# Attention with beacon keys, then an ELU feed-forward: key and query transposes by DMA, loads issued by ScalarE, fillers in the head, smaller first tiles

## The chip, the cores and the metric

The kernel runs on one core of one Trainium2 chip. The metric is the device time of one execution in microseconds (us); it is taken as the median of several runs. The profile is of one execution of its own, with a span from the first to the last instruction and a device time beside it. TensorE is called PE in the profile, VectorE DVE, ScalarE ACT, GpSimd POOL and SyncE SP; SPq, ACTq and POOLq are the instruction queues from which these engines issue DMAs.

## The reference

There are 8 batches of 8 heads, 576 tokens and 64 dimensions per head. 16 beacon keys and values stand ahead of the 576 of each head and are seen by every query; the others are causal. The attention's output, 4608 tokens by 512, goes through a feed-forward of 2048 with an ELU.

```python
scores = (q @ k_all.T) / sqrt(64)              # k_all: 16 beacon keys, then 576 keys
scores[:, 16:] = where(causal, -1e9, scores)   # the beacon columns stay open
a = softmax(scores);  x = a @ v_all            # per batch and head
x = x.transpose(0, 2, 1, 3).reshape(4608, 512)
h = x @ w_in                                   # 512 -> 2048
out = where(h > 0, h, exp(min(h, 0)) - 1) @ w_out
```

## The kernel before

**Attention.** Heads go in pairs: pair n is batch b = n // 4, heads 2·hp and 2·hp + 1. `load_pair` brings keys and queries of a pair into one staging tile `st32` (keys on even partitions, queries on odd), nine consecutive tokens per partition and head, so in rows of 2304 bytes. `cast_pair` makes it bf16 (`st16`), and TensorE transposes it in nine matmuls against an identity, with a tenth for the beacon keys (`do_T`, and `do_T2` for batch 0, which uses other PSUM buffers). VectorE copies the keys from PSUM to `kT` (`do_kT`), VectorE or ScalarE the queries to `qT` (`do_qT`). `do_SC` computes scores with keys on partitions (tile `sc`), `do_exp` applies the exponential on ScalarE (`et`), `do_mask` zeroes the causal part on GpSimd, `do_AV` multiplies by V (`av`, with a column of ones for the sums), and `do_norm` divides into `x16`. From batch 2 on `turn_x` transposes `x16` into `xT` by DMA on SP, five per batch; batches 0 and 1 do it on TensorE (`do_xT`).

V is loaded by `load_v` in five chunks of 128 keys per batch, in rows of 256 bytes, and cast by `cast_v`. Staging buffers: four `st32`, two `st16`, five `vst`, one `bk32` for the beacon keys.

**Feed-forward.** Tokens go in tiles, two of 256 and then eight of 512. `do_mm1` computes 512 columns of `hps` by 4 matmuls of 512 (or 8 of 256) columns; `do_e` (ScalarE), `do_clamp` (GpSimd) and `do_join` (VectorE) make the ELU, and `do_mm2` multiplies by `w_out16` into `ops` for 128 tokens at a time, which VectorE copies to `osb` and SP stores. The weights come by eight DMAs from GpSimd's queue, which cast to fp16 (`load_w`), each after a mask that `W_AFTER` names.

**Order.** Nothing in this is left to a run-time scheduler. `Plan` takes every step as an `Op` with an engine, a key, a duration, what it depends on and which buffers it takes and gives, steps through a modelled time, and emits the instructions of each engine in the order that comes out. PE, DVE, ACT, POOL and SP are engines of this plan, and so is a single server "DMA". The keys come from tables (`SHIFT`, `AT`, `AT0`, `PACES`) that set where each batch and each tile lies. `FIRST` gives the order of the first loads. On the chip each engine runs its instructions in that order and waits for semaphores. DMAs from SP and ScalarE share eight semaphores in turn: a DMA waits until the one eight places before it has landed.

```python
slots = {"sc": 2, "ff": 4, "av": 2, "ops": 1, "et": NET, "rl": 2, "e": NE, "gt": NG, "osb": 3,
         "st": 4, "sb": 2, "bk": 1, "vst": 5}
plan = Plan(slots, {"PE": 16.0})
```

"ff" are the four PSUM buffers that `hps`, `av`, `xt` and `ops` take in turn; "sc" are two double buffers for scores, and for the transposes of `do_T`.

Of the kernel before, what the change touches and what calls it, by code (L numbers as in the profile page):

```python
# [10 lines left out]
FP32 = mybir.dt.float32  # L11
FP16 = mybir.dt.float16
BF16 = mybir.dt.bfloat16
AFT = mybir.ActivationFunctionType
ALU = mybir.AluOpType
P = 128


class Op:
    def __init__(self, eng, key, dur, fn, deps=(), take=(), give=(), mode=None, lat=0.03):  # L20
        self.eng, self.key, self.dur, self.fn = eng, key, dur, fn
        self.deps, self.take, self.give = [d for d in deps if d is not None], take, give
        self.mode, self.lat = mode, lat
        self.left, self.after = 0, []


class Plan:
# [10 lines left out]
    def run(self):  # L38
# [9 lines left out]
        free = dict.fromkeys(pending, 0.0)  # L48
        mode = None
        for op in self.ops:  # L50
            if not op.left:
                heapq.heappush(ready[op.eng], (op.key, op.seq))
        events, order, now, n_left, tick = [], [], 0.0, len(self.ops), 0
        while n_left:
            for eng in ready:
                if free[eng] > now + 1e-9:
                    continue
                line = pending[eng]
# [16 lines left out]
                for item in skipped:  # L75
                    heapq.heappush(ready[eng], item)
                if op is None:
                    continue
                for t in op.take:
# [14 lines left out]
            while events and events[0][0] <= now + 1e-9:  # L94
                _, _, op = heapq.heappop(events)
                if op is None:
                    continue
                n_left -= 1
                for t in op.give:
                    self.slots[t] += 1  # L100
                for o in op.after:
                    o.left -= 1
                    if not o.left:
                        heapq.heappush(ready[o.eng], (o.key, o.seq))
        self.length = now
# [7 lines left out]
def kernel(  # L113
# [23 lines left out]

    TILES = [(0, 256), (256, 512)] + [(t, t + TTS) for t in range(TTS, NT, TTS)]
    NTT = len(TILES)
# [59 lines left out]

    NG, NET, NKQ = 20, 8, 4  # L200
    konst = ctx.enter_context(tc.tile_pool(name="konst", bufs=1))
# [20 lines left out]
    x16s = [big.tile([P, NKC, DM], FP16, name=f"x16_{i}") for i in range(2)]  # L222
    kTs = [big.tile([P, SKP], BF16, name=f"kT_{i}") for i in range(NKQ)]
    qTs = [big.tile([P, S], BF16, name=f"qT_{i}") for i in range(NKQ)]
    et_bufs = [big.tile([P, 2, 512], FP16, name=f"et_{i}") for i in range(NET)]
# [4 lines left out]
    with tc.tile_pool(name="psum", bufs=1, space=bass.MemoryType.PSUM) as psum:  # L230
# [3 lines left out]
            "sc": 2, "ff": 4, "av": 2, "ops": 1, "et": NET, "rl": 2, "e": NE, "gt": NG, "osb": 3,  # L234
            "st": 4, "sb": 2, "bk": 1, "vst": 5,
        }
        plan = Plan(slots, {"PE": 16.0})
        add = plan.add

# [3 lines left out]

        def load(key, dur, fn, deps=(), take=(), issue=0.47):

            issue = add("SP", key, issue, fn, deps=deps, take=take)
            issues.append(issue)
            return add("DMA", key, dur, None, deps=[issue], lat=2.0)

        issues = []  # L250
        add("SP", -1e6, 0.8, None)
# [3 lines left out]
        def load_bk(b):  # L255
            t = bks[b] = stage.tile([P, DM], FP32, tag="bk", name="bk32", bufs=1)
            nc.sync.dma_start(
                out=t[0:NB].rearrange("n (h d) -> n h d", h=H), in_=beacon_k[b].rearrange("h n d -> n h d"))
# [13 lines left out]
        def cast_pair(n, eng):  # L272
# [4 lines left out]
            else:  # L277
                eng.tensor_copy(out=dst, in_=src)  # L278

        def turn_x(b, blk):  # L280
            q0, rows, _ = BLOCKS[blk]
            nc.sync.dma_start_transpose(  # L282
                out=xTa[:, :, b * S + q0:b * S + q0 + rows], in_=x16s[b % 2][0:rows, blk, :])

        def load_v(b, jc):
            vst = vsts[b, jc] = stage.tile([P, H, D], FP32, tag="vst", name="vst", bufs=5)
            if jc == 0:
                nc.sync.dma_start(out=vst[0:NB], in_=beacon_v[b].rearrange("h n d -> n h d"))
            r0 = NB if jc == 0 else 0
            lo = P * jc - NB + r0  # L290
            n = kc_sz[jc] - r0
            nc.sync.dma_start(out=vst[r0:r0 + n], in_=v[b, :, lo:lo + n, :].rearrange("h s d -> s h d"))

# [190 lines left out]
        def do_store(tt, t4):  # L484
# [4 lines left out]

        SHIFT = [18.19, -1.67, -5.21, 9.28, 2.92, -5.56, -3.02, 18.21]  # L490
        AT = [-2.75, -0.54, -0.93, -0.06, 0.2, 1.01, 1.99, -16.61]
        AT0 = [[-45.78, -33.15, -38.79, -34.41], [-45.52, -23.75, -37.77, -41.96], [-33.6, -16.81, -31.44, -41.61]]
        PACES = [(-10.52, 1.48, 24.15, -2.31), (-10.42, 4.31, 27.52, 4.6), (37.71, 0.81, 11.65, 4.01), (83.94, 2.16, 31.7, 1.22), (112.53, 2.24, 29.18, 2.45)]
        W_AFTER = [[21.51, 12.09, 17.39, 6.76], [7.67, 24.47, 24.74, 25.24]]
        ON_POOL = "20010220"
        X_ON_ACT = "00"
        LAG = 17.55
        URGE = 72.32
        Q_ON_ACT = "01111110"
        FIRST = (  # L500
            "q2 k1 q1 v2 v1 k2 k3 q3 q5 v0 q4 k4 k5 v4 b1 v3 k6 q6 v6 v5 v9 q7 k7 v8 v7 ").split()

# [14 lines left out]
        def plan_loads(n):  # L517
            b, hp = divmod(n, HP)
            if hp == 0:
                got = load(load_key(f"b{b}", place(b, 0) - 31), 0.2, partial(load_bk, b), take=["bk"])  # L520
                bk_in[b] = add("POOL", place(b, -0.9), 0.6, partial(cast_bk, b),
                               deps=[got] + last_T.get(b - 2, []), give=["bk"])
                if b == 0:
                    marks.append(bk_in[b])
# [12 lines left out]
        def plan_v(b):  # L537
            for jc in range(NKC):
                key = load_key(f"v{NKC * b + jc}", place(b - 1, 1.8 + 0.4 * jc))
                got = load(key, 1.5, partial(load_v, b, jc), take=["vst"], issue=1.0 if jc == 0 else 0.5)  # L540
                v_cast[b, jc] = add(
                    "DVE", place(b, -0.7 + 0.16 * jc), 0.56, partial(cast_v, b, jc),
                    deps=[got] + last_AV.get(b - 2, []), give=["vst"])

        def plan_w(which, f4):
            after = marks[max(0, min(len(marks) - 1, round(W_AFTER[which][f4])))]
            got = add("POOL", after.key + 0.01, 0.8, partial(load_w, which, f4), deps=[after])
            got = add("DMA", f4 - 300, 3.2, None, deps=[got], lat=2.5)
            w_at.update({(which, 4 * f4 + c): got for c in range(4)})

        def plan_T2(n, key):
# [28 lines left out]
        def plan_pair(n):  # L580
            b, hp = divmod(n, HP)
            at = lambda a: place(b, hp + a)
            key = AT0[0][hp] - 4 if b == 0 else at(AT[1])
            ready = plan_T2(n, key) if b == 0 else plan_T(n, key)
            masked = {}
# [3 lines left out]
            for units, key in steps:  # L589
                SC = add(  # L590
                    "PE", key, sum(0.00024 * 2 * CUT.width[u] + 0.02 for u in units), partial(do_SC, n, units),
                    deps=ready + [SC], take=["sc"] * len(units), mode=1, lat=0.19)
                last_kq[n] = SC
                first_SC.setdefault(n, SC)
                for u in units:
# [12 lines left out]
            for r, groups in enumerate([(0,), (1,), (2,)] if b == 0 else [(0,), (1, 2)]):  # L608
# [11 lines left out]
                if b >= XB:  # L620
                    for blk in blks:
                        part.setdefault(blk, []).append(normed[-1])
                    if hp == HP - 1:
                        for blk in blks:
                            s = add("SP", at(AT[7]), 1.25, partial(turn_x, b, blk), deps=part.pop(blk))
                            done = add("DMA", at(AT[7]), 0.5, None, deps=[s], lat=2.2)
                            last_X.setdefault(b, []).append(done)
# [22 lines left out]
        def plan_tile(p):  # L650
            lo, hi = TILES[p]
            base, pitch1, start2, pitch2 = PACES[p] if p < len(PACES) else (32 * (p - 1) + LAG,) + PACES[-1][1:]
            xs = []
# [18 lines left out]
            for i in range(4 * t4s):  # L672
# [7 lines left out]
                    take=held if f4 == 0 else [],  # L680
                    give=["gt"] * (steps // 8) if t4 == t4s - 1 else [], mode=0, lat=0.19)
                if f4 == 3:
                    osb = add("DVE", key + 0.6, 0.7, partial(do_osb, p, t4), deps=[quarter], take=["osb"], give=held)
                    st = add("SP", key + 0.7, 0.47, partial(do_store, p, t4), deps=[osb])
                    add("DMA", key + 0.7, 1.0, None, deps=[st], give=["osb"], lat=2.0)

        for t in kTs:
            nc.vector.memset(t[:, SK:SKP], 0.0)  # L690
        for t in bk16s:
# [15 lines left out]
        for p in range(NTT):  # L707
            plan_tile(p)
        issues.sort(key=lambda i: i.key)
        add("DMA", -800, 0.7, None, deps=[issues[2]])  # L710
        for one, two in zip(issues, issues[1:]):
            two.deps.append(one)
        plan.run()
# [28 lines left out]
```

## Time and profile before

| | |
|---|---|
| median of 3 runs | 367.61 us (367.36 to 368.18) |
| the profiled execution | 367.97 us |
| its span | 366.2 us, 8353 instructions |
| mean granted TensorE clock | 0.989 |
| PE, DVE, ACT, POOL busy | 346.9, 213.3, 205.3, 190.6 us |
| bytes by DMA | 46.54 MB in 73256 packets, 56321 of them under 512 bytes |

How it is read: the page has the busy time of each engine and the span in 40 slices, each digit a busy share in tenths. Views by stretch give the same in microseconds, with the granted clock and the share of the 16 DMA engines that was busy. The chain of waits goes back from the last instruction to whatever released each step. The timeline lists instructions in order of time, those of one line together; the ends of matmuls are modelled, their starts are not. The DMA view has packets and bytes of a stretch, and the median time from issue to landing.

### The profile page before, as it was taken

How to read it: one execution, taken by the hardware profiler on the slowest of the kernel's cores; microseconds unless marked ns; L12 is line 12 of the kernel's file. 1: busy time of each engine (PE TensorE's matmuls, PEld its weight loads, DVE VectorE, ACT ScalarE, POOL GpSimd, SP SyncE). 2: the span in 40 equal slices, each digit the busy share in tenths (PEclk: the TensorE clock that was granted, in tenths of full speed). 3: DMA queues.
4: the chain of work that ended last, by engine and by line, in shares of the span. 5: the costliest groups of instructions: out<-in, count | busy, mean ns of one | idle time of the engine just before them, and what ended most of it. 6: DMA issues, size and time to landing. Idle time of an engine off the chain costs nothing.

```text
span 366.2 us, 8353 instructions
## 1 busy us (share of the span) xinstructions
PE 346.9 (95%) x3240; PEld 191.7 (52%) x3240; DVE 213.3 (58%) x454; ACT 205.3 (56%) x308; POOL 190.6 (52%) x363
## 2 busy tenths in 40 slices
PE   1796999999999999999999999999999999999995
PEld 1564775755465556555555554544555544444442
DVE  1575367778864777765756765555666554554321
ACT  3775683568857786767677666435546534333100
POOL 3383582658855866757466656335534434344200
PEclk9998799999999999999999999999999999999999
DMA  7999995788137966957696600220000221000022
GB/s 215 295 235 243 235 164 148 179 233 285 55 68 203 273 83 161 208 146 197 143 235 170 135 30 29 57 68 29 31 29 30 57 68 57 30 29 29 30 94 78
DMA packets 73256, 46.54 MB, mean 127 GB/s; under 512 B 56321, under 2 KB 60417, under 8 KB 73217
## 3 DMA queue, kind: packets, MB, share of 16 engines
q1 hardware_dynamic: 68848, 41.53, 43.4%
q0 software_dynamic: 4224, 4.19, 7.0%
q8 instruction: 25, 0.41, 0.5%
q10 hardware_dynamic: 144, 0.29, 0.2%
q14 instruction: 15, 0.11, 0.1%
HBM read 37.22 MB, written 9.44 MB: 127 GB/s over the span
## 4 chain that ended last, share of the span: by engine, by line
PE 86%; DMA 5%; DVE 2%; POOL 2%; ACT 2%; SPq 1%; issue 1%; ACTq 0%; DVEq 0%
PE ops L476 34%; PE hps L449 33%; PE sc L362 7%; PE av L396 7%; PE tr L311 3%; DMA w_in<-in_moe_w_in_dram 3%; DMA st<-in_q_dram 1%; POOL et L377 1%; PE tr L321 1%; DMA vst<-in_v_dram 1%; ACT et L371 1%; DVE kT L345 1%; DVE gt L468 1%; SPq L282 0%; DVE v L296 0%
## 5 line engine op out<-in xcount | busy, mean ns | idle before, releaser
L449 PE MATMUL hps<-xT,w_in 128*128 128x512 f16 (+1 forms) x640 | 146.0, 363 | 2.8 <-DMA w_in<-in_moe_w_in_dram 2.2
L476 PE MATMUL ops<-w_out,gt 128*128 128x512 f16 x576 | 144.2, 379 | 0.0
L468 DVE SCALAR_TENSOR_TENSOR gt<-e,hps 128x512 f16<-128x512 f32 x144 | 97.6, 684 | 79.5 <-POOL e L459 79.3
L459 POOL TENSOR_SCALAR e<-e 128x512 f32<-128x512 f32 x144 | 89.5, 624 | 104.3 <-ACT e L455 101.5
L455 ACT ACTIVATE e<-hps 128x512 f32<-128x512 f32 x144 | 85.5, 599 | 90.8 <-PE hps L449 86.9
L371 ACT ACTIVATE et<-sc 128x800 f16<-128x800 f32 (+3 forms) x128 | 103.9, 864 | 22.0 <-PE sc L362 18.8
L449 PEld LDWEIGHTS <-w_in 128*128 128x128 f16 x640 | 60.5, 99 | 59.3 <-DMA w_in<-in_moe_w_in_dram 2.3
L476 PEld LDWEIGHTS <-gt 128*128 128x128 f16 x576 | 52.4, 98 | 57.5 <-issue 3.0
L377 POOL TENSOR_SCALAR_AFFINE_SELECT et<-et 128x256 f16<-128x256 f16 (+2 forms) x160 | 60.0, 402 | 40.4 <-ACT et L371 37.3
L396 PEld LDWEIGHTS <-et 128*128 128x128 f16 (+1 forms) x960 | 37.3, 100 | 10.8 <-issue 1.9
L396 PE MATMUL av<-v,et 128*128 128x65 f16 (+1 forms) x960 | 41.5, 197 | 0.6 <-POOL et L377 0.6
L362 PE MATMUL sc<-qT,kT 64*128 64x80 bf16 (+3 forms) x704 | 37.2, 238 | 3.4 <-ACT et L371 1.8
L482 DVE COPY osb<-ops 128x512 f32<-128x512 f32 x36 | 24.8, 689 | 23.8 <-PE ops L476 23.6
L362 PEld LDWEIGHTS <-kT 64*128 64x128 bf16 x704 | 21.8, 97 | 25.4 <-issue 19.2
L412 DVE TENSOR_TENSOR x<-av,rl 128x256 f16<-128x256 f32 (+2 forms) x68 | 32.0, 471 | 2.3
L278 POOL CAST st<-st 128x1152 bf16<-128x1152 f32 x25 | 28.7, 1149 | 8.1 <-PE tr L313 6.4
L351 ACT ACTIVATE qT<-tr 128x576 bf16<-128x576 bf16 x24 | 15.6, 649 | 19.8 <-DVE kT L346 12.0
L345 DVE COPY kT<-tr 128x576 bf16<-128x576 bf16 x28 | 21.1, 754 | 8.1 <-PE tr L313 7.7
L411 DVE RECIPROCAL rl<-av 128x4 f32<-128x4 f32 (+2 forms) x68 | 12.5, 183 | 16.6 <-PE av L396 15.5
L296 DVE CAST v<-vst 128x512 f16<-128x512 f32 (+1 forms) x40 | 18.9, 489 | 4.3 <-DMA vst<-in_v_dram 4.3
L311 PEld LDWEIGHTS <-st 128*128 128x128 bf16 x252 | 16.1, 98 | 5.6 <-issue 0.4
L311 PE MATMUL tr<-identb,st 128*128 128x128 bf16 x252 | 18.6, 219 | 0.1
(32 smaller groups left out, 69.0 us busy)
## 6 DMA issues: line engine op xcount, KB each, us to landing
st<-in_k_dram SPq DMA_DIRECT2D x32, 288.0 KB, 4.2
out_dram<-osb SPq DMA_DIRECT2D x36, 256.0 KB, 2.1
st<-in_q_dram SPq DMA_DIRECT2D x31, 288.0 KB, 4.5
vst<-in_v_dram SPq DMA_DIRECT2D x24, 256.0 KB, 5.3
w_in<-in_moe_w_in_dram POOLq DMA_DIRECT2D x4, 512.0 KB, 9.0
w_out<-in_moe_w_out_dram POOLq DMA_DIRECT2D x4, 512.0 KB, 8.4
vst<-in_v_dram SPq DMA_DIRECT2D x8, 224.0 KB, 4.0
vst<-in_v_dram SPq DMA_DIRECT2D x8, 160.0 KB, 5.0
```

The source lines that it names most:

```text
L278: eng.tensor_copy(out=dst, in_=src)
L311: nc.tensor.transpose(out=tr[:, P * g:P * g + P], in_=b16s[n][:, g].rearrange("p h d -> p (h d)"), identity=identb)
L362: nc.tensor.matmul(out=sc[:, h, o:o + w], lhsT=kT[D * h:D * h + D, P * jc:P * jc + P], rhs=qT[D * h:D * h + D, q0:q0 + w], start=True, sto ...
L371: nc.scalar.activation(out=et[:, :, 0:w], in_=scs[n, u][:, :, 0:w], func=AFT.Exp, bias=0.0, scale=float(1.0 / (D ** 0.5)))
L377: nc.gpsimd.affine_select(out=et[:, :, c0:c0 + dw], in_=et[:, :, c0:c0 + dw], compare_op=ALU.is_ge, fill=fill0, base=q0 + NB - P * jc, pat ...
L396: nc.tensor.matmul(out=av[:, c:c + D + 1], lhsT=ets[n, CUT.unit_of[jc, at]][0:m, h, col:col + P], rhs=v16[0:m, jc, 2 * hp + h, 0:D + 1], s ...
L412: nc.vector.tensor_tensor(out=x16s[b % 2][:, blks[0]:blks[0] + nb, P * hp:P * hp + P].rearrange("q i (h d) -> q i h d", d=D), in0=av[:, :, ...
L449: nc.tensor.matmul(out=hps[:, (hi - lo) * j:(hi - lo) * (j + 1)], lhsT=w_in16[:, cc, P * fc:P * fc + P], rhs=xT[cc][:, lo:hi], start=(cc = ...
L455: nc.scalar.activation(out=e, in_=hpss[tt, i], func=AFT.Exp, bias=0.0, scale=1.0)
L459: nc.gpsimd.tensor_scalar(out=e, in0=e, scalar1=1.0, scalar2=0.0, op0=ALU.min, op1=ALU.max)
L468: nc.vector.scalar_tensor_tensor(out=gt, in0=es[tt, i], scalar=1.0, in1=hpss[tt, i], op0=ALU.subtract, op1=ALU.max)
L476: nc.tensor.matmul(out=ops, lhsT=gts[tt, fc][:, P * t4:P * (t4 + 1)], rhs=w_out16[:, fc, :], start=(fc == 0), stop=(fc == NFC - 1))
```

## The change

Six things are changed together.

1. From batch 3 on (`PE_B = 3`) keys and queries are no longer transposed on TensorE. `load_tok` brings 128 tokens by 512 (all eight heads) in rows of 256 bytes, two chunks to a staging tile; `cast_tok` makes them bf16 on VectorE or GpSimd (table `TOK`); `turn_tok` transposes each chunk by DMA on SP straight into `kT` or `qT`, which now hold a whole batch, two of each. Per batch there are five chunks of keys and five of queries, so 50 more DMA transposes.
2. From batch 3 on the loads of queries and of V are issued by ScalarE (`ON_ACT = "011"`), those of keys by SP.
3. Where TensorE has nothing to do in the plan's first 30 us, it gets a filler: a matmul of 256 columns on a tile of ones, into a buffer that nobody reads.
4. The first feed-forward tile of 256 tokens becomes two of 128.
5. The plan's model of DMA: three queues served in turn, and a limit on what SP and ScalarE may have outstanding ("ringSP", "ringACT").
6. The tables, and some buffers: `NG` 18 for 20, `vst` 4 for 5 with the beacon keys in it too, a new `FIRST`, and `W_AFTER` with all four quarters of w_in after the first beacon cast.

```diff
-    TILES = [(0, 256), (256, 512)] + [(t, t + TTS) for t in range(TTS, NT, TTS)]
+    TILES = [(0, 128), (128, 256), (256, 512)] + [(t, t + TTS) for t in range(TTS, NT, TTS)]
...
-    kTs = [big.tile([P, SKP], BF16, name=f"kT_{i}") for i in range(NKQ)]
+    kTa = [big.tile([P, HP, SKP], BF16, name=f"kT_{i}") for i in range(2)]
...
+                    if eng == "PE" and now < self.fill_until and self.slots["ff"]:
+                        order.append((now, len(order), self.filler))
...
+        def do_fill():
+            spare = psum.tile([P, 512], FP32, tag="ff", name="spare", bufs=4)
+            nc.tensor.matmul(out=spare[:, 0:2 * P], lhsT=ones[:, 0:P], rhs=ones, start=True, stop=True)
+        plan.fill_until, plan.filler = 30.0, Op("PE", 0, 0.12, do_fill)
...
+        def load_tok(b, is_k, c, eng):
...
+            eng.dma_start(out=t[r0:r0 + n], in_=(k if is_k else q)[b, :, lo:lo + n, :].rearrange("h s d -> s h d"))
+        def turn_tok(b, is_k, c):
+            r0, n, lo = rows_of(is_k, c)
+            t = (kTa if is_k else qTa)[b % 2]
+            nc.sync.dma_start_transpose(
+                out=t[:, :, P * c:P * c + r0 + n],
+                in_=b16s[b, is_k, c // 2].rearrange("p g h d -> p (g h d)")[0:r0 + n, DM * (c % 2):DM * (c % 2) + DM])
...
-        W_AFTER = [[21.51, 12.09, 17.39, 6.76], [7.67, 24.47, 24.74, 25.24]]
+        W_AFTER = [[-82.55, -95.08, -88.46, -80.14], [10.13, 13.03, 11.82, 22.08]]
+        TOK = ("011010", "100110", "010101", "110100", "001100")
+        ON_ACT = "011"
...
-                got = load(key, 1.5, partial(load_v, b, jc), take=["vst"], issue=1.0 if jc == 0 else 0.5)
+                on, eng = QUEUES[ON_ACT[2] == "1" and b >= PE_B]
+                got = load(key, 1.3, partial(load_v, b, jc, eng), take=["vst"], issue=1.2 if jc == 0 else 0.6, units=8, on=on)
...
-            ready = plan_T2(n, key) if b == 0 else plan_T(n, key)
+            ready = plan_T2(n, key) if b == 0 else plan_T(n, key) if b < PE_B else turned[b]
...
+            if b >= PE_B:
+                plan_tok(b)
             for hp in range(HP):
-                plan_loads(b * HP + hp)
+                if b < PE_B:
+                    plan_loads(b * HP + hp)
```

More of the change, by code (lines that the diff above doesn't have):

```diff
@@ L242, with load @@
         qk_in, v_in, v_cast = {}, {}, {}
[L244 to L250, printed above, removed]
+        def load(key, dur, fn, deps=(), take=(), issue=0.47, units=1, on="SP"):
+            ring = ["ring" + on] * units
+            issue = add(on, key, issue, fn, deps=deps, take=take + ring)
+            issues[on].append(issue)
+            if "vst" not in take:
+                issues["st"].append(issue)
+            return add("DMA", key, dur, None, deps=[issue], lat=2.0, give=ring, queue=0 if on == "SP" else 2)
+        issues = {"SP": [], "ACT": [], "st": []}
         add("SP", -1e6, 0.8, None)
@@ L255, in load_bk @@
         def load_bk(b):
-            t = bks[b] = stage.tile([P, DM], FP32, tag="bk", name="bk32", bufs=1)
+            t = bks[b] = stage.tile([P, H, D], FP32, tag="vst", name="bk32", bufs=4).rearrange("p h d -> p (h d)")
             nc.sync.dma_start(
@@ L708 @@
             plan_tile(p)
[L709 to L712, printed above, removed]
+        for line in issues.values():
+            line.sort(key=lambda i: i.key)
+            for one, two in zip(line, line[1:]):
+                two.deps.append(one)
+        add("DMA", -800, 0.7, None, deps=[issues["SP"][2]])
         plan.run()
```

128 lines of the change are left out of this document (96 added, 32 removed).

## The prediction

> **What bounds the kernel now.** I read the page first, then the busy time by stretches, then the chain that ended last, and last the timelines of TensorE and of SP's queue.
>
> ```profile
> PE 346.9 (95%) x3240; PEld 191.7 (52%) x3240; DVE 213.3 (58%) x454; ACT 205.3 (56%) x308; POOL 190.6 (52%) x363
> PE   1796999999999999999999999999999999999995
> PEclk9998799999999999999999999999999999999999
> DMA  7999995788137966957696600220000221000022
> ```
>
> TensorE is busy in nearly every slice after the fifth, the other engines in little over half. The DMA row is full at the start, half full in the middle, nearly empty at the end. The stretches separate these:
>
> ```profile
> core 0: us, PE busy (x) PEld busy (x) DVE busy (x) ACT busy (x) POOL busy (x), PEclk, DMA share, GB/s
> 27.00:36.00 9.00, 5.83 (x110) 4.38 (x108) 4.86 (x21) 4.91 (x6) 3.58 (x8) 0.90 1.20 243
> 36.00:45.00 9.00, 9.00 (x72) 6.77 (x71) 2.31 (x4) 4.92 (x8) 4.52 (x9) 0.72 1.04 243
> 91.00:110.00 19.00, 19.00 (x204) 10.49 (x204) 13.86 (x30) 13.52 (x21) 13.34 (x25) 1.00 0.24 61
> 146.00:164.00 18.00, 18.00 (x186) 9.68 (x183) 12.69 (x30) 12.06 (x19) 12.73 (x22) 1.00 0.75 183
> ```
>
> Until 36 us TensorE waits, beside DMAs that never pause; from 36 to 45 us it is busy at a granted clock of 0.72; after that it has no idle time. What it does in the steady part is a sum of instructions, and a removed instruction is time saved. The head is a matter of what arrives when.
>
> ```profile
> 0.84 4.65 DMA st<-in_q_dram
> 23.90 11.63 DMA w_in<-in_moe_w_in_dram
> 35.57 5.30 PE hps L449 x24
> 41.42 3.60 PE hps L449 x32
> 65.47 1.46 PE av L396 x48
> 344.90 17.28 PE ops L476 x80
> ```
>
> The chain says that the first feed-forward matmuls start at 35.57 us because a quarter of w_in lands then. They run at 0.221 us each (5.30/24), those from 41.42 us at 0.1125 (3.60/32): half the clock until then. The last matmul ends at 362.2 us (344.90 + 17.28), so 4.0 us of the 366.2 us span are the last copy and store. A 512-column matmul is 0.216 us (17.28/80), one of attention times V 0.0304 (1.46/48).
>
> ```profile
> 145.16 0.67 PE L311 MATMUL tr<-identb,st 128*128 128x128 bf16 x9
> 145.66 0.22 PE L313 MATMUL tr<-identb,bk 128*128 128x128 bf16 x1
> 145.71 0.35 PE L396 MATMUL av<-v,et 128*128 128x65 f16 x6
> ...
> 146.76 1.03 PE L476 MATMUL ops<-w_out,gt 128*128 128x512 f16 x4
> 147.72 0.52 PE L362 MATMUL sc<-qT,kT 64*128 64x256 bf16 x14
> 148.17 1.90 PE L449 MATMUL hps<-xT,w_in 128*128 128x512 f16 x8
> 150.00 0.55 PE L362 MATMUL sc<-qT,kT 64*128 64x240 bf16 x8
> 150.49 0.90 PE L396 MATMUL av<-v,et 128*128 128x65 f16 x24
> ```
>
> Starts are to be read here, since ends are modelled. Ten transposes take 145.71 − 145.16 = 0.55 us of TensorE. The two score groups of a pair take 0.45 and 0.49 us, and the four matmuls ahead of a group 0.96 instead of 0.864, so 0.10 more each: 1.14 us per pair.
>
> **The sum for TensorE.** Before: 1088 matmuls of 512 columns × 0.216 = 235.0; 128 of 256 × 0.1125 = 14.4; 320 transposes × 0.055 = 17.6; 960 × 0.0304 = 29.2; 32 pairs × 1.14 = 36.5; 40 small transposes of x at about 0.05 = 2. Together 334.7 us at full clock. First matmul at 6.8 us, tail 4.0: the remaining 20.7 us of the span are waits and half clock, nearly all ahead of 42 us.
>
> After, from the order in which the built program's instructions stand: 20 pairs (batches 3 to 7) lose ten transposes each, 20 × 0.55 = 11.0 us saved, all in the part with no idle time. The first 256-token tile becomes two of 128: 64 matmuls of 256 columns (7.2 us) turn into 128 of 128 columns, which I price like the transposes of the same width (7.0 us): nothing. So 323.5 us of needed work. To this come 120 fillers of 256 columns, all in the first 30 us or so, 51 of them ahead of the first transpose.
>
> **The head.** The fillers wait for one VectorE memset and so start at about 1.1 us:
>
> ```profile
> 0.88 0.17 DVE L690 MEMSET kT<- 128x24 uint32 x4 [0.88 <-PEq L726]
> 16.01 1.14 PE L321 MATMUL tr<-identb,st 128*128 128x128 bf16 x9 [0.55 <-POOL st L278]
> 16.94 0.31 PE L324 MATMUL tr<-identb,bk 128*128 128x128 bf16 x1
> ```
>
> The second and third row show 0.103 us per transpose (0.93/9) at 16 us against 0.055 later: the head now runs at half clock, though the page's clock row marks its first slices 9. With fillers the clock should rise early. They cost 120 × 0.11 = 13.2 us, or twice that if the clock never rose; I take half clock for the first 5 us, 2.5 us more. The Trainium skill's page "TensorE: Matmul & The Clock Gate", section "Part 1: The HAM clock gate", gives about 3.4 us of sustained work until full clock; by that the surcharge would be an estimated 1.7 us and the whole sum 0.8 us lower. The trace before can't decide it: its head is too sparse to show a warm-up. The second fall of the clock, seen in the 36 to 45 us row behind a TensorE wait, goes if the fillers and the earlier tile keep TensorE fed.
>
> So without a wait other than the fillers, the span is 1.1 + 323.5 + 13.2 + 2.5 + 4.0 = 344.3 us. By the same prices 21.9 us of work and fillers stand ahead of the first feed-forward matmul; with 1.1 and 2.5 it starts near 25 us instead of 35.57. Is its data there? The first tile now needs only 128 queries, so V chunks 0 and 1, and the first w_in quarter; all w_in quarters are freed for issue by the first beacon cast, with two masks and a cast of GpSimd standing ahead of them, so at 12 to 14 us. That leaves batch 0's loads their queue until then. The second to fourth quarter come while batch 1's loads run beside them; I add 3 us of waits (0, if each quarter lands in time, to 12, the rival below).
>
> **The steady part: what replaces the transposes.** The loads turn from 2304-byte rows into 256-byte rows, and 50 DMA transposes join the 30 of before. Four windows of DMA price them: V rows of 256 B alone (8 to 9 us), pair rows alone (10 to 12), V beside weights (25 to 29, with the page's median of all V loads under it), two transposes (235 to 237.2).
>
> ```profile
> DMA packets 1014, 0.26 MB, mean 259 GB/s; under 512 B 1012, under 2 KB 1012, under 8 KB 1014
> ```
> ```profile
> DMA packets 353, 0.72 MB, mean 362 GB/s; under 512 B 39, under 2 KB 39, under 8 KB 353
> ```
> ```profile
> vst<-in_v_dram SPq DMA_DIRECT2D x1, 256.0 KB, 17.3
> ...
> vst<-in_v_dram SPq DMA_DIRECT2D x24, 256.0 KB, 5.3
> ```
> ```profile
> q1 hardware_dynamic: 1023, 0.25, 56.8%
> xT<-x SPq DMA_TRANSPOSE x2, 2.4
> ```
>
> Per batch, k and q were 8 × 288 KB at 362 GB/s, 6.5 us; they become 9344 packets at 1014 per us, 9.2 us, and ten transposes at 0.62 us (0.568 × 2.2 / 2), 5.7 us after short last chunks. With V (4.7), x transposes (2.8) and stores (4.5 × 0.7 at the pair rows' rate, 3.2) DMA work grows from 17 to some 26 us per batch, and TensorE needs (323.5 − head)/8, about 36 us. It fits, at some 70%. These are long chains, though: load, cast, transpose, and the first score matmul of a batch waits for all ten transposes. By counting the TensorE work that stands between a batch's last cast and its first score matmul I get 5.2, 4.4, 5.4, 6.1 and 6.9 us for batches 3 to 7. Against that stand a cast (about 0.5 us, half of the row below for half the data), SP's issue, and the landing:
>
> ```profile
> L278 POOL CAST st<-st 128x1152 bf16<-128x1152 f32 x25 | 28.7, 1149 | 8.1 <-PE tr L313 6.4
> 103.39 6.51 SPq L282 DMA_TRANSPOSE xT<-x  x5
> 110.64 0.63 SPq L269 DMA_DIRECT2D st<-in_k_dram  x1
> 145.41 3.28 SPq L292 DMA_DIRECT2D vst<-in_v_dram  x3
> 168.13 3.32 SPq L292 DMA_DIRECT2D vst<-in_v_dram  x3
> ```
>
> Issue is 1.3 us (6.51/5), landing 2.4: 4.2 us, just inside. If everything ahead is 3 us late, each of the five batches loses up to 3 us: 0 to 15 us; I take 4, nearer the low end, since by the same count a chain starts some 27 us ahead. SP's queue carries 15 transposes × 1.3 and some 10 loads and stores × 0.63, 26 us per batch, in order, with stores waiting for VectorE among it: busy, not full. The copies from PSUM (kT on VectorE, qT on ScalarE) go, casts on VectorE and GpSimd stay about as many; none of these engines has over 14 of 19 us busy above, so I price that at nothing; if this cover were gone it would show as waits of score matmuls.
>
> Queries and V from batch 3 on are issued by ScalarE: 55 issues at 0.63, 35 us on an engine with 160 us idle. The exponentials stand behind each. The Trainium skill's page "DMA: Bandwidth & Descriptors", section "Rules for kernel authors", holds that spreading DMAs over issuing engines brings no bandwidth and saves issue time alone. By that the move buys SP 0.63 × 11 = 7 us per batch and nothing more. This trace, with one load issued by ScalarE, can't show it. My sum counts no gain for the move.
>
> **Sum.** 344.3 + 3 + 4 = 351.3 us of span. The profiled run is 367.97 us for 366.2 of span, and the median of the runs is 367.61: 1.4 more than the span. Forecast 352.7 us, which I round to 353; its own range without a rival is 346 (no waits) to 358.
>
> **Rivals.**
> (1) V meets the weights. The row of 17.3 us shows what a V load takes beside weight traffic, against 5.3 otherwise. TensorE's order puts the attention over V chunks 2 to 4 ahead of the first feed-forward matmul. If the weights start before those three loads are through, the feed-forward work starts near 35 us as now, and 10 us are lost: 363 us. For it: both want the same 10 us of DMA. Against: weights stand behind GpSimd's masks. Chance 0.12.
> (2) Late transposes: 3 us at each of five batches, DMA and SP's order being behind the plan: 353 + 11 = 364 us. For it: 4.2 us against gaps of 4.4 to 6.9. Against: DMA has a quarter of its time free. Chance 0.15.
> (3) The other side: ScalarE's queue blocks. A full queue or a semaphore still held by an older DMA makes an issue wait, and every exponential behind it, and then TensorE. SP's rows at 145.41 and 168.13 show three issues in 3.3 us, 0.5 us more each than 0.63. On SP that cost nobody. If TensorE pays 0.5 for each of 55, it is 27 us: 353 + 27 = 380 us. It decides from (367.6 − 353)/55 = 0.27 us per issue on. Against: ScalarE is idle 44% of the time, and four PSUM buffers lie between. Chance 0.1.
> (4) The change doesn't do what it says in the head: fillers delay real work, or the clock stays low; only 11.0 us minus waits are won: 366.2 − 11.0 + 4 + 1.4 = 360.6 us. Chance 0.08.
>
> **How the numbers follow.** The forecast has 0.55. Range 346.5 to 364: it takes in the forecast's own range, and rivals 1, 2 and 4 up to their prices; the slow case is left out. About 0.2% is what a measurement of this kernel can tell from no change. Faster 0.88 (all but rival 3 and a rest), same 0.02, slower 0.10.
>
> **What would show it.** Right: TensorE without L311-like transposes in steady stretches, feed-forward matmuls from about 25 us at 0.056 us each, granted clock 1.00 from some 6 us on, and no waits longer than 1 us at the first scores of batches 3 to 7. Wrong: score matmuls released by DMA for several us per batch (rival 2); exponentials idle behind ScalarE's own DMA issues (3); average of V landings above 15 us in the first 30 us, with the first hps near 35 us (1). A span under 344 would refute the sum itself, as the fillers can't be skipped.

## The result, and the profile after

The changed kernel takes 365.47 us (median of 20 runs, 363.76 to 368.63), the kernel before 368.06 us beside it (20 runs): a ratio of 0.9941, 95% interval 0.9921 to 0.9962. It is faster by 0.6%, where 353 us, 4%, had been forecast; the result lies above the range's end of 364.0. The profiled execution took 366.9 us for a span of 365.2, against 366.2 before. Medians here and below are of all executions of a kernel, while the ratios and their intervals leave out the few that were over 1.5% slower than the kernel's fastest.

From the page of the profile after: busy times, and the rows of TensorE, its clock and the DMA engines in 40 slices.

```profile
PE 347.6 (95%) x3224; PEld 190.6 (52%) x3224; DVE 206.4 (57%) x431; ACT 189.1 (52%) x281; POOL 183.2 (50%) x357
PE   8999589899998899999999999999999999999995
PEclk9999989999999899999999999999999999999999
DMA  7999997547799889699999999999300411000022
```

TensorE is busy from the first slice now, fillers included. There are two dents, in the fifth slice and around the thirteenth, and the DMA row is full from there to two thirds of the way, where it was half empty. The same by stretches, two more of them than before:

```profile
27.00:36.00 9.00, 8.41 (x161) 7.18 (x160) 6.68 (x23) 5.55 (x8) 6.53 (x12) 1.00 1.19 232
36.00:45.00 9.00, 5.33 (x89) 4.48 (x86) 2.84 (x9) 5.90 (x9) 5.62 (x10) 1.00 1.21 208
45.00:54.00 9.00, 6.80 (x72) 5.79 (x73) 6.38 (x14) 3.12 (x5) 4.63 (x9) 0.81 1.03 234
91.00:110.00 19.00, 19.00 (x158) 9.30 (x156) 11.62 (x23) 10.16 (x16) 10.19 (x20) 1.00 1.00 177
110.00:128.00 18.00, 15.26 (x164) 8.04 (x163) 5.88 (x15) 8.55 (x13) 6.20 (x15) 0.91 0.92 153
146.00:164.00 18.00, 18.00 (x170) 9.04 (x168) 10.86 (x22) 11.11 (x17) 11.43 (x22) 1.00 0.89 178
```

The head's wait has moved from ahead of 36 us to behind it. The steady part, idle-free before, has a hole of 2.7 us and a slower clock at 110 to 128 us.

How far had each kernel come by 73 us? TensorE's groups of the first 73 us, counts behind the x, first of the kernel before (feed-forward, scores, attention times V), then of the one after (its two views: all forms of `hps` apart, then the attention's groups):

```profile
L449 PE MATMUL hps<-xT,w_in 128*128 128x256 f16 x128 | 17.8, 300 | 2.8 <-DMA w_in<-in_moe_w_in_dram 2.2 <-DVE gt L468 0.7
L476 PE MATMUL ops<-w_out,gt 128*128 128x512 f16 x46 | 11.6, 380 | 0.0
L362 PE MATMUL sc<-qT,kT 64*128 64x80 bf16 (+3 forms) x176 | 11.6, 266 | 2.9 <-ACT et L371 1.8 <-DVE kT L338 1.1
L396 PE MATMUL av<-v,et 128*128 128x65 f16 (+1 forms) x216 | 10.7, 209 | 0.6 <-POOL et L377 0.6
```
```profile
L516 PE MATMUL hps<-xT,w_in 128*128 128x256 f16 x64 | 9.0, 291 | 0.7 <-DVE gt L535 0.7
L516 PE MATMUL hps<-xT,w_in 128*128 128x128 f16 x128 | 8.7, 224 | 0.6 <-DVE gt L535 0.6
...
L543 PE MATMUL ops<-w_out,gt 128*128 128x512 f16 x12 | 3.1, 380 | 0.0
...
L516 PE MATMUL hps<-xT,w_in 128*128 128x512 f16 x4 | 1.0, 379 | 0.0
```
```profile
L463 PE MATMUL av<-v,et 128*128 128x65 f16 (+1 forms) x246 | 10.8, 193 | 4.6 <-DVE gt L535 4.6
L429 PE MATMUL sc<-qT,kT 64*128 64x80 bf16 (+3 forms) x198 | 10.3, 229 | 0.8 <-DVE qT L420 0.7
```

By the prediction's prices the old kernel had done 128 × 0.1125 + 46 × 0.216 = 24.3 us of feed-forward work by then, the new one 64 × 0.1125 + 128 × 0.055 + 16 × 0.216 = 17.7. In attention the new one is ahead by 30 × 0.0304 and 22 × 0.052 (36.5 us over 704 score matmuls), 2.1 us, and by some 0.5 us of transposes. So **the new head ends about 4.1 us behind the old one**, although its first feed-forward matmul starts at 28.04 us instead of 35.57. From 73 us on, the new kernel needs 292.2 us and the old one 293.2: 4.1 us more to do and 11.0 less for transposes should have made that 6.9 less. So **5.9 us of waits and lower clock have come into the steady part**. 4.1 − 11.0 + 5.9 = −1.0, the difference of the spans.

Where the head waits, in the chain that ended last, then in TensorE's timeline (a bracket holds the idle time before and its releaser):

```profile
24.40 20.93 DMA vst<-in_v_dram
45.34 0.02 issue
45.36 0.43 DVE v L363
45.78 0.61 DVE gt L535
46.39 0.14 issue
46.53 0.34 PE av L463 x6
```
```profile
28.04 1.06 PE L516 MATMUL hps<-xT,w_in 128*128 128x128 f16 x16
...
41.41 0.55 PE L429 MATMUL sc<-qT,kT 64*128 64x240 bf16 x8
46.53 0.34 PE L463 MATMUL av<-v,et 128*128 128x65 f16 x6 [4.58 <-DVE gt L535]
46.71 1.08 PE L378 MATMUL tr<-identb,st 128*128 128x128 bf16 x9
```

The view names `gt`, but `gt` stood on VectorE behind the cast `v`, and that behind a V load of batch 1 that took 20.93 us beside the weights. Nine transposes behind the 4.58 us wait take 1.08 us instead of 0.67: the clock has fallen, and the stretch of 45 to 54 us has it at 0.81, so (1 − 0.81) × 9 / 0.5 = 3.4 us at half.

The hole of the steady part, in the timelines of ScalarE and TensorE:

```profile
118.42 0.39 ACTq L330 DMA_DIRECT2D st<-in_q_dram  x1
119.24 0.81 ACT L438 ACTIVATE et<-sc 128x768 f16<-128x768 f32 x1 [4.00 <-DMA xT<-x]
```
```profile
120.10 0.34 PE L429 MATMUL sc<-qT,kT 64*128 64x240 bf16 x4 [2.22 <-ACT et L438]
```

An exponential stands behind a query load of batch 4 that ScalarE issues, and the load waits until a DMA transpose of x on SP has landed (they share the eight semaphores). TensorE's score buffers stay full for those 2.22 us.

### The profile page after: what moved, and what is told of

Its sections match the earlier page's. It is cut to its first block, busy times and chain, and to the rows that moved or that the text cites. A ratio compares the mean times of both kernels' runs of the same rounds, so it can differ in the third digit from the quotient of the medians.

```text
span 365.2 us, 8339 instructions
## 1 busy us (share of the span) xinstructions
PE 347.6 (95%) x3224; PEld 190.6 (52%) x3224; DVE 206.4 (57%) x431; ACT 189.1 (52%) x281; POOL 183.2 (50%) x357
## 4 chain that ended last, share of the span: by engine, by line
PE 75%; DMA 15%; DVE 4%; ACT 2%; POOL 2%; issue 1%; SPq 1%; ACTq 0%; DVEq 0%; POOLq 0%
PE ops L543 30%; PE hps L516 28%; DMA vst<-in_v_dram 7%; PE sc L429 6%; PE av L463 5%; DMA st<-in_k_dram 4%; PE spare L268 4%; DMA xT<-x 1%; DVE gt L535 1%; DMA kT<-st 1%; DMA qT<-st 1%; ACT et L438 1%; POOL e L526 1%; SPq L343 1%; PE tr L378 1%
## 5 line engine op out<-in xcount | busy, mean ns | idle before, releaser
L516 PE MATMUL hps<-xT,w_in 128*128 128x512 f16 (+2 forms) x704 | 144.3, 343 | 1.3 <-DVE gt L535 1.3
L516 PEld LDWEIGHTS <-w_in 128*128 128x128 f16 x704 | 62.4, 99 | 59.4 <-issue 2.6
L463 PEld LDWEIGHTS <-et 128*128 128x128 f16 (+1 forms) x960 | 36.7, 98 | 16.2 <-issue 7.0
L429 PE MATMUL sc<-qT,kT 64*128 64x80 bf16 (+3 forms) x704 | 35.5, 228 | 4.1 <-ACT et L438 2.9
L429 PEld LDWEIGHTS <-kT 64*128 64x128 bf16 x704 | 20.9, 95 | 24.6 <-issue 21.1
L268 PE MATMUL spare<-ones 128*128 128x256 bf16 x120 | 19.4, 299 | 1.8 <-DVE ones L784 1.3
L336 POOL CAST st<-st 128x1024 bf16<-128x1024 f32 (+2 forms) x14 | 13.2, 944 | 7.5 <-DMA st<-in_k_dram 7.3
L268 PEld LDWEIGHTS <-ones 128*128 128x128 bf16 x120 | 12.1, 107 | 5.8 <-issue 1.4
L313 POOL CAST st<-st 128x1152 bf16<-128x1152 f32 x10 | 11.7, 1165 | 4.3 <-DMA st<-in_q_dram 4.2
L336 DVE CAST st<-st 128x1024 bf16<-128x1024 f32 (+2 forms) x16 | 11.1, 692 | 3.9 <-DMA kT<-st 1.5
## 6 DMA issues: line engine op xcount, KB each, us to landing
w_in<-in_moe_w_in_dram POOLq DMA_DIRECT2D x4, 512.0 KB, 12.5
```

What stands on the lines that cost most here:

```text
L268: nc.tensor.matmul(out=spare[:, 0:2 * P], lhsT=ones[:, 0:P], rhs=ones, start=True, stop=True)
L429: nc.tensor.matmul(out=sc[:, h, o:o + w], lhsT=kT[D * h:D * h + D, P * jc:P * jc + P], rhs=qT[D * h:D * h + D, q0:q0 + w], start=True, sto ...
L463: nc.tensor.matmul(out=av[:, c:c + D + 1], lhsT=ets[n, CUT.unit_of[jc, at]][0:m, h, col:col + P], rhs=v16[0:m, jc, 2 * hp + h, 0:D + 1], s ...
L516: nc.tensor.matmul(out=hps[:, (hi - lo) * j:(hi - lo) * (j + 1)], lhsT=w_in16[:, cc, P * fc:P * fc + P], rhs=xT[cc][:, lo:hi], start=(cc = ...
```

## The experiments

All times are medians, and ratios are to the kernel before, run beside each; what is taken off or added is counted from the changed kernel's 365.47 us.

**The parts, one at a time.** First the issues of part 2 back on SP:

```diff
-        ON_ACT = "011"
+        ON_ACT = "000"
```

> All loads issued by SP again; the DMA transposes and everything else as in the changed kernel. Theory A: ScalarE's loads wait for a semaphore that an SP transpose still holds (at 118.42 us ScalarE's query load waited for an x transpose, ScalarE stood 4.0 us and TensorE 2.2), so without them the TensorE waits between 110 and 125 us go: about 4 us less, 361.5 us. Rival B: the chain of load, cast and transpose on SP is what is late; SP gets 11 more issues per batch at 0.6 us, so the same waits stay or grow: 365 to 372 us.

Measured: 419.62 us, ratio 1.1438 (1.1382 to 1.1494). Neither theory: 54 us worse. TensorE's waits, in all, times, longest:

```profile
PE sc L429 <- DMA qT<-st: 24.8, 5, 7.6
PE av L463 <- DVE v L363: 18.4, 6, 5.1
```

SP's queue runs in order, and loads that could go stand there behind stores and transposes that wait for copies and casts:

```profile
SPq L553 <- DVE osb L549: 77.1, 14, 11.8
SPq L343 <- DVE st L336: 24.5, 6, 6.4
```

The plan orders everything anew when the issuing engine changes, so the 54 us are of the queue and of the new order together. With this set of tables the DMA transposes don't pay without ScalarE's issuing.

Then parts 1 and 2 undone, the rest kept:

```diff
-    PE_B = 3
+    PE_B = 8
```

> PE_B = 8: all batches are transposed on TensorE again (and so all loads are in pair form and on SP); fillers, tiles of 128, tables and weights order as in the changed kernel. It prices the head and the steady part apart. Theory A: the changed kernel won 11.2 us by the 200 transposes, lost 5.5 to waits behind ScalarE and SP in the steady part and 3.7 in the head: this kernel has 11.2 more work and no 5.5, so 371 us, 3.5 over the kernel before. Rival: the head is a gain and the steady part eats it: then this is at or under 365.

Measured: 374.38 us, 1.019 (1.0148 to 1.0233), 3.4 above theory A. No wait from 70 us on is over 1 us, and the head's wait for V is there as before, 4.8 us. That points to a changed head that is a loss by itself, as the count at 73 us says: 6.3 us here against 4.1 there. The order is one of its own, to which I put the other 2 us without having shown it.

The opposite: DMA transposes and ScalarE's loads with every table of the kernel before and no fillers, then the same with fillers until 38 us of the plan:

```diff
-    TILES = [(0, 128), (128, 256), (256, 512)] +
+    TILES = [(0, 256), (256, 512)] +
... (SHIFT, AT, AT0, PACES, W_AFTER, FIRST and the rest as before)
-        plan.fill_until, plan.filler = 30.0,
+        plan.fill_until, plan.filler = 0.0,      # second kernel: 38.0
```

> Only the DMA transposes from batch 3 on, the ScalarE loads and the plan's new model of DMA, with every table of the kernel before (tiles, paces, weights, first loads) and no fillers. The emitted order is a new one. Theory A (the new head costs what the transposes save): the first feed-forward matmul stays near 35 us, steady transposes save 11, new waits cost 5.5: 362 us, faster than the changed kernel. Rival (head and steady part are tied: without the new head the new loads of batch 3 come late): waits in the first scores of batch 3, 367 us or more.

> The same as the run with DMA transposes alone, with fillers where TensorE has nothing to do until 38 us of the plan. If the half clock of the head costs time (before: half until 27 us and from 34 to 41 us), 3.4 us faster than without fillers, about 359 us. If the head waits for data anyway, as the run of the changed kernel without its fillers showed, the same within 1 us.

Measured: 388.92 us, 1.0578 (1.0541 to 1.0614), and 392.85 us, 1.0664 (1.0614 to 1.0713). The steady part of the first, by stretches:

```profile
128.00:230.00 102.00, 87.75 (x823) 43.76 (x822) 52.55 (x111) 54.90 (x81) 51.00 (x98) 0.95 0.90 168
```

14 us idle and the clock at 0.95. My reading, which no run shows, is that the old tables give the longer chains of loads no lead. The DMA transposes don't pay with these old tables, so the change can't be split into a good half and a bad half by tables. With fillers the time is 3.9 us more instead of 3.4 less, again in an order of its own.

Three runs that were meant to undo single pieces of the head changed the plan's whole order, as the runs above do, and say little. Fillers left out of the plan:

> No fillers; all else as in the changed kernel. Theory A (the head waits for DMA, and the fillers fill that wait): 365 to 367 us, within 1.5 us of the changed kernel, with the transposes of batch 0 at about 0.105 us each instead of 0.055. Rival C (the clock in the head sets the time): the first 25 us of work at half clock cost 6 us or more: 371 us.

Measured: 371.77 us, 1.0072 (1.0035 to 1.011). `W_AFTER` of the kernel before:

> The weights' issue times are those of the kernel before (W_AFTER), all else as in the changed kernel. Theory A: V of batch 1, which took 20.9 us to land beside the weights, lands within 10 us; the first feed-forward matmul moves back from 28 to about 36 us, but TensorE's 4.6 us wait at 42 us and the half clock behind it go: 361 to 365 us. Rival D (early weights are what makes the head quick): the feed-forward's later start is lost: 371 us or more.

Measured: 392.34 us, 1.0694 (1.0657 to 1.0731), with TensorE idle for 14.3 us between 36 and 73 us and for 8.5 us more until 128 us. The head's tables of the kernel before among the other new ones:

> The head of the kernel before (two tiles of 256, its first loads, its keys for batch 0 and its weights' times, no fillers) with the DMA transposes and ScalarE's loads from batch 3 on. Theory A (the head change costs 4 to 6 us, the transposes win 11.2 and give back 5.5): 368 - 11.2 + 5.5 = 362 us. Rival G (the steady part alone is worth nothing, the order does it all): 368 us or more.

Measured: 375.21 us, 1.0181 (1.0127 to 1.0234). In all three theory A missed and the time lies where the rival had put it; but all three mix tables of one set with those of another, and so can't tell the rival's cause from a worse order. The runs under the next three headings keep the order of every engine.

**Fillers.** The plan places them, and nothing is emitted:

```diff
         def do_fill():
-            spare = psum.tile([P, 512], FP32, tag="ff", name="spare", bufs=4)
-            nc.tensor.matmul(out=spare[:, 0:2 * P], lhsT=ones[:, 0:P], rhs=ones, start=True, stop=True)
+            return
```

> Same order of instructions as the changed kernel, with the 120 fillers left out of it. Theory A (fillers take the place of waits): within 2 us of the changed kernel, 364 to 368 us; the head's transposes and scores run at half clock. Rival F (fillers delay real work: 51 stand ahead of the first transpose, which started at 9.05 us against 6.79 before): 3 us or more less, 362 us. Rival C (without fillers the clock sets the head): 370 us or more.

Measured: 365.41 us, 0.9941 (0.9911 to 0.9972): the same as with them. TensorE comes to V of batch 1 2 us earlier, and waits longer:

```profile
39.47 0.55 PE L428 MATMUL sc<-qT,kT 64*128 64x240 bf16 x8
48.20 0.49 PE L462 MATMUL av<-v,et 128*128 128x65 f16 x6 [8.18 <-DVE gt L534]
```

120 fillers are neither a cost nor a gain here: without them TensorE waits longer for the landing of the same V load.

**ScalarE's hold.** Only batch 4's first two query loads are issued by GpSimd:

```diff
+            eng = nc.gpsimd if (b, is_k) == (4, False) and c < 2 else eng
```

> The first two query loads of batch 4 are issued by GpSimd instead of ScalarE; the order of every engine stays that of the changed kernel. Theory B (ScalarE is held at 113 to 118 us because these loads must wait for a semaphore that a transpose on SP still holds, exponentials stand behind, TensorE waits 2.8 us and then runs 3.4 us at half clock): ScalarE's 4.0 us of idle time behind xT<-x at 119 us and TensorE's wait of 2.2 us at 120 us are gone, the clock stays full from 110 to 128 us, 3 to 4.5 us faster than the changed kernel: 361.0 to 362.5 us. Rival (the transposes and loads are late anyway, the hold only shows it): the wait turns up elsewhere within 10 us, above 364.5 us.

Measured: 365.48 us, 0.9945 (0.9918 to 0.9972). The hold at 118 us is gone, and no time is won by the medians. What is left of ScalarE's idle time just ahead of that place, 3.50 us, is no new hold: it stands in the changed kernel too (first row; the second is of this run):

```profile
108.36 1.70 ACT L438 ACTIVATE et<-sc 128x736 f16<-128x736 f32 x2 [3.50 <-DMA st<-in_k_dram]
109.67 1.70 ACT L439 ACTIVATE et<-sc 128x736 f16<-128x736 f32 x2 [3.50 <-DMA vst<-in_v_dram]
```

It costs TensorE nothing in either. TensorE's idle time from 73 to 350 us is 4.4 us here and 4.2 in the changed kernel; it has moved into later waits of at most 0.9 us, most of them further off than the 10 us that the rival named. In this execution the head's wait for V was also 6.5 us instead of 4.58, which an edit at 113 us can't cause, so one profile doesn't close the balance. The medians (12 and 20 runs) speak for the rival's time.

**Bytes.** Weight DMAs that bring a quarter:

```diff
-                dst, src = w_in16[:, :, 512 * f4:512 * f4 + 512], moe_w_in[:, 512 * f4:512 * f4 + 512]
+                dst, src = w_in16[:, :, 512 * f4:512 * f4 + 128], moe_w_in[:, 512 * f4:512 * f4 + 128]
... (w_out likewise; the matmuls read the quarter that is there)
```

> Same order of instructions as the changed kernel, but the eight weight DMAs bring a quarter of the columns, and the feed-forward reuses that quarter (so three quarters of both weights are left out of the computation; matmuls are as many and as long). Theory A (batch 1's V stands 20.9 us beside the weights' packets, and TensorE's 4.6 us wait at 42 us and the half clock behind it come from that): V of batch 1 lands within 8 us, both go, and the waits between 50 and 70 us shrink too: 8 us less than the changed kernel, about 357.5 us. Rival E (the waits of the head come from the chains between engines or from the order itself): 364 us or more.

Measured: 360.44 us, 0.9782 (0.9717 to 0.9848; 4 runs): 5.0 off, and the 4.6 us wait with them. Theory A had 8; the waits between 54 and 73 us, 1.3 us, did not shrink. The same in the kernel before, as a control:

> The kernel before with weight DMAs that bring a quarter, as a control. Its first feed-forward matmul waited for a quarter of w_in until 35.57 us. Theory A (head bound by data in both kernels): the old head gains more than the new, 5 to 10 us: 358 to 363 us, so that lighter weights do not single out the change. Rival (the old head waits for pairs and copies, not for weights): 366 us or more.

Measured: 362.25 us, 0.9838 (0.9808 to 0.9868), 5.8 below the 368.06 of the kernel before. The weights' bytes cost both heads 5 to 6 us, the old one no less; so V beside the weights is what the new head waits for, but not what makes it worse than the old.

Loads of batches 3 to 7 that bring one head of eight:

```diff
-            eng.dma_start(out=t[r0:r0 + n], in_=(k if is_k else q)[b, :, lo:lo + n, :].rearrange("h s d -> s h d"))
+            eng.dma_start(out=t[r0:r0 + n, 0:1], in_=(k if is_k else q)[b, 0:1, lo:lo + n, :].rearrange("h s d -> s h d"))
... (V and the beacons likewise; the casts read the one head eight times)
```

> From batch 3 on the loads of keys, queries and V bring one head of eight (an eighth of the bytes and packets), and the casts spread it over all eight; the outputs of batches 3 to 7 are therefore those of one head's data. Orders, issues, DMA transposes and matmuls are the changed kernel's. Theory A (late data is the cost in the steady part): TensorE's waits from 70 us on (5.5 us with their half clock) are gone, 360.0 us. Rival B (issues, semaphores and transposes are the cost, not bytes): the 118 us hold stays, above 363.5 us.

Measured: 359.64 us, 0.9777 (0.9742 to 0.9812), 5.8 off, as theory A said. Its stretches:

```profile
36.00:54.00 18.00, 12.09 (x161) 10.24 (x159) 9.20 (x23) 9.02 (x14) 10.21 (x19) 0.91 1.11 216
110.00:128.00 18.00, 17.99 (x212) 9.37 (x206) 10.48 (x23) 12.47 (x17) 9.09 (x20) 1.00 0.50 103
128.00:350.00 222.00, 222.00 (x1747) 109.84 (x1746) 123.67 (x235) 115.04 (x174) 105.96 (x200) 1.00 0.31 73
```

The head is untouched, the steady part without a gap, though every issue, semaphore and DMA transpose is still there. Median landing times between 80 and 270 us, of the changed kernel and of this one:

```profile
st<-in_q_dram ACTq DMA_DIRECT2D x18, 256.0 KB, 4.7
...
kT<-st SPq DMA_TRANSPOSE x25, 3.8
...
xT<-x SPq DMA_TRANSPOSE x25, 4.2
```
```profile
st<-in_q_dram ACTq DMA_DIRECT2D x18, 32.0 KB, 2.0
...
kT<-st SPq DMA_TRANSPOSE x25, 2.5
...
xT<-x SPq DMA_TRANSPOSE x25, 2.5
```

The full loads slow the transposes beside them, from 2.5 to 3.8 and 4.2 us, and the prediction had priced the chain with the unloaded 2.4.

Both kinds of bytes:

> The same, and each weight DMA brings a quarter (matmuls read that quarter again and again, outputs are those of a quarter of the weights). If late bytes explain all that the forecast missed but 2.4 us of work and 0.7 of fillers: 365.5 - 5 - 5.5 = 355 us. If the two overlap or something else holds: 358 us or more.

Measured: 354.19 us, 0.9626 (0.96 to 0.9653): 11.3 off, where the two alone gave 5.0 + 5.8 = 10.8. They add up, within the spread of the runs. TensorE is busy for 16.2 us of the stretch in which the changed kernel had 5.33 + 6.80 = 12.1, at full clock:

```profile
36.00:54.00 18.00, 16.17 (x237) 13.41 (x236) 14.64 (x34) 12.89 (x20) 13.94 (x26) 1.00 0.62 146
```

**A better version.** w_out later; the plan's order shifts with it in many places:

```diff
-        W_AFTER = [[-82.55, -95.08, -88.46, -80.14], [10.13, 13.03, 11.82, 22.08]]
+        W_AFTER = [[-82.55, -95.08, -88.46, -80.14], [28, 32, 30, 36]]
```

> The four w_out quarters are issued later (marks 28, 32, 30, 36 instead of 10 to 22; GpSimd's issues move from between batch 0's masks to behind batch 1's first ones), w_in as in the changed kernel; the plan orders the rest anew. Theory A: V of batch 1 no longer stands beside w_out and lands within 12 us, TensorE's 4.6 us wait goes; 3 to 6 us less: 360 to 362 us. Rival E: as the changed kernel or worse, 365 us or more, the waits only moving.

Measured: 363.45 us, 0.986 (0.9793 to 0.9926; 4 runs), between theory and rival. With the two query loads on GpSimd as well:

> Later marks for w_out (as in the run with w_out at 28 to 36) and the first two query loads of batch 4 issued by GpSimd. If head collision and ScalarE's hold are two separate costs, 363.5 - 3 = 360.5 us; if the second only moves, 363.5 us.

Measured: 363.76 us, 0.9877 (0.9835 to 0.9918): the two don't add, as if the second again only moved. Later still, marks 38, 42, 40, 44:

> The marks of w_out at 38, 42, 40, 44 instead of 28, 32, 30, 36 (and 10 to 22 in the changed kernel). If w_out beside batch 1's V was all of the head's extra cost, no more than with 28 to 36: 363.5 us, with w_out now late for the second matmuls at some price; if batch 2's loads gain too, 361.5 us.

Measured: 378.94 us, 1.0302 (1.027 to 1.0333). The price of a late w_out, which the expectation left open, is one wait:

```profile
PE ops L543 <- DMA w_out<-in_moe_w_out_dram: 13.5, 1, 13.5
```

So w_out at 28 to 36 beats the kernel before, and the changed one by about 2 us, though less surely: its interval just touches the changed kernel's, and that of the kernel with the two loads on GpSimd lies below it.

## Why the prediction was wrong

**The step that failed is the head**, in the words "I add 3 us of waits". The sum put 1.1 + 13.2 + 2.5 + 3 = 19.8 us of the new head in place of 6.8 + 20.7 = 27.5 of the old, a gain of 7.7. The count at 73 us shows a loss of 4.1: 11.8 us missed, so by the count 14.8 us stand in the place of the 3. Of these, 8.3 are TensorE's idle time between its first matmul and 73 us (8.0 in the old kernel, so that none of it was won) and 1.7 the half clock behind the wait for V; the other 4.8 are not taken apart. Behind the 3 us stands a thought that was not tested: that an earlier first feed-forward matmul is earlier work done. The DMA row is full for the head in both kernels, and the two runs with light weights gained 5.0 and 5.8 us, so both heads wait for bytes. TensorE did its first 128-token tiles earlier and then waited for V of batch 1. Fillers were priced as the cost of a faster clock; emptied, they changed nothing, so neither the price nor the gain showed in the time.

**Rival 1 named the right collision at the wrong place.** It looked at V chunks 2 to 4 of batch 0 ahead of 25 us. Those held up little; batch 1's V at 24 to 45 us did not, with the first `hps` at 28.04 and not near 35. That the price of 10 us lies near the 11.8 missed is luck. Rival 4 was right that the head gains nothing, but neither of the causes that it names is seen: without the fillers the time is the same, and the clock does rise. Why the new head is worse than the old one by 4.1 us is only half settled: w_out moved back gives 2.0 of it at most (its order shifts as well); the rest I could not take apart, since the other edits of the head changed the whole order.

**The steady part was mis-sized by 2 us.** 4 us were allotted, from 0 to 15; 5.9 by the count, and 5.8 by the run with light loads. TensorE's idle time from 73 us on, 4.2 us, and the half clock between 110 and 128 us, 1.6, make 5.8 as well. The step behind it is "It fits, at some 70%" and, in rival 2, "DMA has a quarter of its time free". Between 80 and 270 us SP's queue (q1) and ScalarE's (q10) take this share of the 16 DMA engines:

```profile
q1 hardware_dynamic: 62289, 19.82, 60.8%
q10 hardware_dynamic: 45520, 11.44, 35.7%
```

Together that is 96.5%; with light loads the same rows have 36.5% and 4.4%. The cause of the lateness is the one given ("DMA and SP's order being behind the plan"), but not its place: no first score matmul waits for a DMA transpose. At its largest place, 118 us, the lateness reaches TensorE through ScalarE, by rival 3's mechanism: an exponential behind an issue that waits. Rival 3's price, 27 us, was far too high, and the hold is not the cause: taken away there, TensorE's idle time came back in others, and it went with the bytes.

**What held.** The 11.0 us of transposes, by the balance of the spans: 4.1 by the count, 5.8 of waits and half clock, and 1.0 us less in all leave 10.9 for them. The filler surcharge: 51 fillers stand between 1.26 and 9.05 us,

```profile
1.26 7.95 PE L268 MATMUL spare<-ones 128*128 128x256 bf16 x51 [1.26 <-DVE ones L784]
9.05 0.67 PE L388 MATMUL tr<-identb,st 128*128 128x128 bf16 x9
```

7.79 − 51 × 0.1125 = 2.1 us against 2.5 predicted. In the trace about the first 21 of them start 0.213 us apart and the others 0.109, so the half clock lasts some 4.5 us, where 5 were taken. The estimate of 1.7 us went by the 3.4 us in the Trainium skill's "TensorE: Matmul & The Clock Gate", "Part 1: The HAM clock gate"; the trace has a little more.

**What agrees by luck.** Freed of late bytes, the kernel takes 354.19 us, 1.2 above the forecast. But the forecast held 7 us of waits (3 + 4) that such a kernel should not have: its sum without them is 344.3 us of span, and the run with both kinds of light bytes has 352.5. Of the 8.2 us between, 5.6 are idle time that TensorE still has there, 4.3 of it ahead of 73 us; the other 2.6 are not taken apart. So late bytes explain 11.3 of the 12.5 us by which the forecast fell short, and the sum was low as well.

**ScalarE's issuing was put at nothing.** I had cited the Trainium skill's "DMA: Bandwidth & Descriptors", "Rules for kernel authors", for spreading DMAs saving issue time alone, and counted no gain. With the loads back on SP the kernel took 54 us more, in a new order, so that this isn't the price of the queue alone. That spreading brings no bandwidth isn't contradicted; that it saves issue time alone doesn't fit the waits in SP's queue there. ScalarE's queue has an order of its own, so that a load needn't stand behind a transpose that waits.

## What to carry to other kernels

Before you count idle time in a head as a gain, ask what ends it: if the DMA row is full there, an earlier start of the work may only move the wait, as here, and fillers may cost and bring nothing. When an operation moves from an engine to DMA, ask whether the queues still have free time, and price its chain with the landing times under the new load, not with those of a quiet trace. To settle such a case, keep the order of all engines and take the bytes away: here the parts then added up, while tables mixed from two plans told little.

## What the runs showed of the hardware

One 256 KB load of V in 256-byte rows took 20.9 us beside the weight loads that cast; the 15 such loads that ScalarE issues, from batch 3 on, had a median of 4.4 us. The granted clock fell to half for about 3.4 us behind a TensorE wait of 4.58 us, and in the stretch of 110 to 128 us (0.91, 3.2 us at half) behind one of only 2.22 us with a short one after it; the second I had not expected. A DMA issued by ScalarE waits for a semaphore that a transpose on SP holds, 4.0 us here, and so an engine that was never short of time stopped TensorE.
